# Wider logit and list products, the first slot's turn placed behind the newest logits, and 16 more routing steps ahead of it

## The chip, the cores and the metric

One core of a Trainium2 chip. The metric is the device time of one execution in microseconds, as the median of repeated runs; before the change it is 1103.21 us (three runs, 1103.02 to 1106.22).

## The reference

Two stages. A causal convolution over 8 sequences of 2880 rows of 192 values, with 7 taps that are a softmax of `weight`, one set for each of 8 heads of 24 columns. Then a mixture of experts over the 23040 rows: the group (of 4) with the largest logit, within it the expert (of 4) with the largest logit, the expert's two layers, and the result scaled by both softmax weights.

```python
out = np.einsum('hk,bskhg->bshg', w, x_unf)              # convolution, w = softmax(weight)
g_idx = np.argmax(x @ w_group, axis=1)
e_idx = np.argmax(xg @ w_expert[g], axis=1)
h  = np.maximum(xg[mask_e] @ w1[g, e], 0.0)              # 192 -> 1024
ye = h @ w2[g, e]                                        # 1024 -> 192
out[tok_idx] = (g_w * e_w)[:, None] * ye
```

## The kernel before

**Routing.** The rows are cut into blocks of 120 and the blocks into 18 units (of 4, 8, 12, 8, 8, 8 and then 12 blocks). `unit` is a generator that writes one unit's work stage by stage: eight conv products, one for a head, with a banded matrix as weights (L505); transposes of the convolved rows (L526, L537); the logits (`logits`, L595 and L600); DVE's choice of group and expert; two small products that count rows per expert (L678, L679); one-hot factors `ohl` and `ohv` on DVE; the list product (L725), which sums over the blocks of the unit to a 128 x 32 table of row numbers per expert; and a POOL DMA that writes the table to `idtab` (L731). The last six units take their logits in another way (`logits_thin`, L580). The convolved rows go to `xcd` in HBM.

**Logits.** In `logits(q)`, a quad of four blocks makes two groups of products: one of the last 64 columns of two blocks against 2 x 20 router weights (L595), and for each of the two blocks one of its first 128 columns against 20 (L600). All the logits of a unit lie in one PSUM bank `lp` (20 columns a block), and DVE reads them by a maximum (L638) and a difference (L639).

**Slots.** A slot runs up to 256 (later up to 384) rows of one expert through its two layers. `gather` (L813) fetches the rows named in the table to `xg`; `turn` transposes them on PE (L831, L833), and makes a high half `xa[:, 0]` on ACT (L844, L847) and a low half `xa[:, 1]` on DVE (L848, L851). `hidden` is the first layer: per pair of 128-column pieces ten products (L864), a high half on ACT (`hh`, L869) and a low half on DVE (`hl`, L870). `back` is the second layer (L882, L886), `finish` scales and writes the rows out.

**Order.** `step()` advances the oldest of the running units by one stage. First, steps are taken until five units are routed; then the first table is read and slots 0 and 1 are gathered (`open_slot`), `AHEAD` more steps are written, then the turn of slot 0, and then the loop over the slots, in which `advance` mixes in steps at a rate that is worked out from the steps already done. The framework's scheduler puts the instructions of each engine into a final order from the order written, priorities and simulated times; engines work through their queues in that order. `tc.high_priority` raises what is written inside it, and `tc.issue_after(ins)` places it behind another instruction in that order.

Of the kernel before, what the change touches and what calls it, by code (L numbers as in the profile page):

```python
# [20 lines left out]
P = 128  # L21
BT = 120
# [5 lines left out]
LH = 32  # L28
# [7 lines left out]
def conv_moe_kernel(  # L36
# [10 lines left out]
    nc = tc.nc  # L47
# [26 lines left out]
    NL = G + E  # L74
# [21 lines left out]
    for b in range(B):  # L96
        k = b * NB
# [14 lines left out]
    QGA = 0  # L112
    QGL = 5
    QGB = 3
    AHEAD = 96
    LISTLAG = 8
    LISTLAG0 = 2
    HOLD = 4
# [207 lines left out]
    for g in range(NSK):  # L326
        nc.sync.dma_start(
            out=skew[0:R, g * HG:(g + 1) * HG],
# [17 lines left out]
    for h in range(H):  # L346
        nc.scalar.activation(
            out=band[0:R, h, 0:BT], in_=skew[0:R, h, BT - 1::-1], func=AF.Exp, bias=wm[0:R, h:h + 1],
# [6 lines left out]
    wr = const.tile([P, 3, NL], F32, name="wr")  # L355
# [20 lines left out]
    def widen_weights():  # L376
# [9 lines left out]
        out=tri, in_=ones, pattern=[[1, P]], compare_op=ALU.is_gt, fill=0.0, base=0, channel_multiplier=-1,  # L386
# [10 lines left out]
    for nb in sorted({n for _, n in units}):  # L397
# [32 lines left out]
        out=sel[:, 0:E], in_=ident.rearrange("p (e l) -> p e l", e=E), axis=AX.X, op=ALU.add)  # L430
    nc.gpsimd.iota(io[:, 0:1], pattern=[[0, 1]], base=0, channel_multiplier=1)
    nc.vector.tensor_scalar(
        out=io[:, 1:2], in0=io[:, 0:1], scalar1=LE - 1, scalar2=None, op0=ALU.bitwise_and)
# [8 lines left out]
        out=eold[:, :, E:E + 1], in_=goff.unsqueeze(1).broadcast_to([P, NU + 1, 1]))  # L442
# [15 lines left out]
    def gaps(u):  # L458

        return tuple(UG[4 * u:4 * u + 4]) if 4 * u < len(UG) else (GA, GL, GB, REST)  # L460
# [17 lines left out]
    def unit(u, pre=None):  # L478
        c0, nb = units[u]
# [3 lines left out]
        def bank(kind=None):  # L483
            if BK and kind and len(unit_banks) > 1:
                pool, nm = BKS[BK][kind]
                return pool.tile([P, 512], F32, name=nm)
            npool[0] += 1
            pool, nm = unit_banks[npool[0] % len(unit_banks)]
            return pool.tile([P, 512], F32, name=nm)
# [10 lines left out]
        for h in range(H):  # L500
            if h:
# [4 lines left out]
                out=ps[0:CW, 0:nb * HC], lhsT=band[0:R, h, 0:CW], rhs=xin[0:R, :, c0h:c1h], start=True, stop=True))  # L506
# [79 lines left out]
        lps = []  # L586

        def logits(q):
            if not lps:
                lps.append(bank("l"))  # L590
            lp = lps[0]
            ta, tb = parts[q][:, 0:QN], parts[q][:, QN:QN + QN // 2]
            for i in range(QB // 2):
                b = q * QB + 2 * i
                nc.tensor.matmul(  # L595
                    out=lp[0:BT, b * NL:(b + 2) * NL], lhsT=tb[:, i * BT:(i + 1) * BT],
                    rhs=wr[:, 1:3].rearrange("p k n -> p (k n)"), start=b == 0, stop=False,
                )
                for k in range(2):
                    nc.tensor.matmul(  # L600
                        out=lp[0:BT, (b + k) * NL:(b + k + 1) * NL], lhsT=ta[:, (2 * i + k) * BT:(2 * i + k + 1) * BT],
                        rhs=wr[:, 0], start=False, stop=b + k == nb - 1,
                    )

        ga, gl, gb, rest = gaps(u)
        events = {}
        for q in range(NQ):
            if thin:
                tl = 1 + APART * q
                todo = ((tl, parts_a), (tl + 1, parts_b), (tl + 4, cross), (tl + 4 + CROSS, logits_thin))  # L610
            else:
                tl = ga + gl + 2 * (NQ - 1) + q
                todo = ((ga + 3 * q, turn_a), (ga + 1 + 3 * q, turn_b), (tl, logits))
            for k, f in todo:
                events.setdefault(k, []).append((f, q))
# [5 lines left out]
        Q = BT  # L621
# [6 lines left out]
        if not thin:  # L628
# [12 lines left out]
            out=sc, in0=dd, scalar=0.0, in1=prio[0:Q].unsqueeze(1).broadcast_to([Q, M, EG]),  # L641
# [5 lines left out]
        ohv = oh.rearrange("p (b m) e -> p b m e", m=NG)  # L647
# [3 lines left out]
            out=ohx[0:Q], in0=ohv[:, :, 1:NG, :].rearrange("p b g e -> p g e b"),  # L651
# [36 lines left out]
        with nc.allow_low_precision(reason="small whole numbers, summed in float32"):  # L688
            nc.vector.tensor_reduce(out=pn[0:Q], in_=pos[0:Q].rearrange("p e b -> p b e"), axis=AX.X, op=ALU.add)
        nc.vector.tensor_scalar(  # L690
            out=posi[0:Q, 0], in0=pn[0:Q], scalar1=LH.bit_length() - 1, scalar2=None, op0=ALU.logical_shift_right)
# [3 lines left out]
        ohl = pa.tile([P, UB // 2, P, 2], BF16, name="ohl", bufs=1)  # L695
        ohr = rt.tile([P, UB // 2, LH, 2], BF16, name="ohr", bufs=1)
        ohv = rt.tile([P, UB // 2, LH, 2], F16, name="ohv")

        def wide(a, n):
# [3 lines left out]
            out=ohr[0:Q, 0:nb // 2], in0=ior[0:Q].unsqueeze(1).broadcast_to([Q, nb // 2, LH, 2]),  # L703
# [3 lines left out]
            out=ohv[0:Q, 0:nb // 2], in0=ohr[0:Q, 0:nb // 2],  # L707
# [3 lines left out]
            out=ohl[0:Q, 0:nb // 2], in0=iop[0:Q].unsqueeze(1).broadcast_to([Q, nb // 2, P, 2]),  # L711
# [10 lines left out]
            yield  # L722
        pl = bank("l")
        for b in range(nb):
            nc.tensor.matmul(out=pl[:, 0:LH], lhsT=ohl[0:Q, b // 2, :, b % 2], rhs=ohv[0:Q, b // 2, :, b % 2], start=b == 0, stop=b == nb - 1)  # L725
        none = rt.tile([P, LH], F32, name="none", bufs=1)
        lsi = rt.tile([P, LH], I32, name="lsi", bufs=4)
        nc.vector.tensor_scalar(out=none, in0=pl[:, 0:LH], scalar1=0.0, scalar2=float(BIG), op0=ALU.is_equal, op1=ALU.mult)
# [1 line left out]
            out=lsi, in0=pl[:, 0:LH], scalar=float(t0 + IDB), in1=none, op0=ALU.add, op1=ALU.add)  # L730
        nc.gpsimd.indirect_dma_start(  # L731
            out=TABV, out_offset=bass.IndirectOffsetOnAxis(ap=rowi.bitcast(U32), axis=0), in_=lsi, in_offset=None,
# [3 lines left out]

    loads = []
    lows = []

    def weights(r1, r2, eng=None, held=False):  # L740
        eng = eng or {}
# [78 lines left out]
    def turn(got, w=SLOT):  # L820
        xs, side = got
        rows = xs.rearrange("p t d -> p (t d)")
        n = -(-w // P)
        xa = ff.tile([P, 2, WMAX], F32R, name="xa")
        xb = xbs[nturn[0] % 2]
        nturn[0] += 1
        px = pm.tile([P, 512], F32, name="pm")
        py, o = (px, SLOT) if n <= 2 else (pm.tile([P, 512], F32, name="pm"), 0)
        for t in range(n):
            a = t * XW + (D2 if side and t == 1 else 0)  # L830
            nc.tensor.transpose(px[:, t * P:(t + 1) * P], rows[:, a:a + P], ident)  # L831
            if not side:
                nc.tensor.transpose(py[0:D2, o + t * P:o + (t + 1) * P], xs[:, t, WB:XW], ident)  # L833
            elif t == 1:
                nc.tensor.transpose(py[:, o:o + P], rows[:, WB:WB + P], ident)
            elif t == 2:
                nc.tensor.transpose(py[0:D2, o + P:o + 2 * P], xs[:, t, WB:XW], ident)
        if side:
            parts = [(0, P, py[0:D2, o:o + P], 0), (P, P, py[D2:P, o:o + P], D2)]
            if w > SLOT:  # L840
                parts.append((SLOT, w - SLOT, py[0:D2, o + P:o + P + w - SLOT], 0))
        else:
            parts = [(0, w, py[0:D2, o:o + w], 0)]
        nc.scalar.activation(out=xa[:, 0, 0:w], in_=px[:, 0:w], func=AF.Copy)  # L844
        for c, k, pb, _ in parts:
            for h in (0, D2):
                nc.scalar.activation(out=xb[h:h + D2, 0, c:c + k], in_=pb, func=AF.Copy)  # L847
        nc.vector.tensor_tensor(  # L848
            out=xa[:, 1, 0:w], in0=px[:, 0:w], in1=xa[:, 0, 0:w].bitcast(F32), op=ALU.subtract)
        for c, k, pb, h in parts:  # L850
            nc.vector.tensor_tensor(  # L851
                out=xb[0:D2, 1, c:c + k], in0=pb, in1=xb[h:h + D2, 0, c:c + k].bitcast(F32), op=ALU.subtract)
        return xa, xb
# [276 lines left out]
    def step():  # L1130

        if routed[0] < NU and len(live) < lead[1] and (not live or max(live, key=lambda a: a[0])[1] >= (lead[0] and lead[0] + (SKEWX if routed[0] > THIN else 0) or SK[min(routed[0], len(SK)) - 1])):
            u = routed[0]
            live.append([u, 0, unit(u, xin0 if u == 0 else None)])
            routed[0] += 1
        if not live:
            return
        done[0] += 1
        cur = live.pop(0)
        cur[1] += 1  # L1140
        try:
            next(cur[2])
            live.append(cur)
        except StopIteration:
            pass
# [103 lines left out]
    opened, gathered, turned = {}, {}, {}  # L1249
# [36 lines left out]
    k = 0  # L1286
# [13 lines left out]
    for e in range(2, 2 + PRE2):  # L1300
        pre[e] = weights(e * D, e * F)
    for k in range(AHEAD):
        step()
# [5 lines left out]
        split_one(opened[0][0])  # L1309
    unit_banks[:] = [(pm, "pm")]  # L1310
    lead[:] = SKEW2, LIVE2
    turned[0] = turn(gathered[0])
    pinned[0] = False
    pend = []
    ends = []
# [68 lines left out]
    for i, (pi, e, s) in enumerate(plan):  # L1384
# [13 lines left out]
        for f2 in range(NF // 2):  # L1398
            last = f2 == NF // 2 - 1
# [66 lines left out]
```

## Time and profile before

| | before |
|---|---|
| median of the runs (three) | 1103.21 us |
| the profiled execution's own time | 1095.27 us |
| its span, first to last instruction | 1093.5 us |
| mean granted clock of TensorE | 0.98 |
| PE busy | 1054.8 us (96%) |
| weight loads (PEld) busy | 1027.2 us (94%) |
| DVE busy | 746.6 us (68%) |
| ACT busy | 668.4 us (61%) |
| POOL busy | 524.3 us (48%) |

The profile shows one execution; engines run side by side, so busy times don't add up. "PEclk" is the granted clock as a share of 2.4 GHz: 0.50 is 1.2 GHz. In a row of instructions in time order, the number in brackets is how long the engine stood idle before it and what ended that.

### The profile page before, as it was taken

What the parts mean: (1) busy time and instruction counts of PE and PEld (TensorE: products, weight loads), DVE (VectorE), ACT (ScalarE), POOL (GpSimd) and SP (SyncE); (2) the same over time, 40 slices, a digit from 0 to 9 for tenths busy, and PEclk for the clock granted to TensorE, in tenths of its full rate; (3) what the DMA queues carried; (4) which work ended last, traced back from release to release, by engine and by line L of the source; (5) the groups of instructions that cost most, each with busy time, mean ns of one, the idle gap of its engine ahead of it and who ended that gap; (6) DMA issues with size and microseconds to landing.
All of it is one profiled execution on the core that took longest, in us unless ns stands there. A gap on an engine that the chain in (4) does not pass through costs nothing. (4 is left out here: it accounts for less than half of the span.)

```text
span 1093.5 us, 22348 instructions
## 1 busy us (share of the span) xinstructions
PE 1054.8 (96%) x7908; PEld 1027.2 (94%) x7908; DVE 746.6 (68%) x1790; ACT 668.4 (61%) x1486; POOL 524.3 (48%) x485
## 2 busy tenths in 40 slices
PE   5988999988999999999999999999999999999996
PEld 5868899988999999999999999999999999999996
DVE  3664887888797887886876665656666656566553
ACT  5454676666576666566667665666566656566552
POOL 2014133344455464565555656455555645465432
PEclk9977899999999999999999999999999999999999
DMA  8999679898797785655645432423333332323210
GB/s 186 239 208 245 147 172 222 210 213 221 172 229 179 172 188 107 142 146 129 121 114 130 127 102 81 110 71 101 103 92 101 100 93 73 91 80 100 62 31 26
DMA packets 193540, 148.55 MB, mean 136 GB/s; under 512 B 84635, under 2 KB 178883, under 8 KB 193422
## 3 DMA queue, kind: packets, MB, share of 16 engines
q1 hardware_dynamic: 127392, 92.90, 35.0%
q0 software_dynamic: 19392, 36.09, 12.9%
q10 hardware_dynamic: 46638, 18.07, 7.9%
q8 instruction: 63, 1.03, 0.4%
q14 instruction: 55, 0.45, 0.1%
HBM read 100.48 MB, written 36.47 MB: 125 GB/s over the span
## 5 line engine op out<-in xcount | busy, mean ns | idle before, releaser
L882 PE MATMUL po<-cw,hh 128*128 128x384 f32 x944 | 295.5, 370 | 0.4 <-ACT ys L940 0.4
L864 PE MATMUL ph<-xa,ah 128*128 128x256 f32 x944 | 260.5, 297 | 7.1 <-DVE hl L870 4.7
L869 ACT ACTIVATE hh<-ph 128x512 fp32r<-128x512 f32 x236 | 140.4, 597 | 179.3 <-PE ph L864 158.8
L886 PE MATMUL po<-cw,hl 128*128 128x192 f32 x944 | 237.1, 251 | 0.0
L870 DVE SCALAR_TENSOR_TENSOR hl<-ph,hh 128x512 fp32r<-128x512 f32 x236 | 161.0, 687 | 106.9 <-ACT hh L869 105.1
L813 POOL DMA_INDIRECT xg<-xcd,idpt x137 | 145.4, 1061 | 176.3 <-ACT ys L940 74.3
L813 POOL DMA_INDIRECT xg<-xcd,idp x116 | 131.8, 1136 | 189.7 <-ACT ys L940 94.9
L864 PEld LDWEIGHTS ph<-xa,ah 128*128 128x128 f32 x944 | 179.5, 190 | 10.9 <-DVE hl L870 5.5
L864 PE MATMUL ph<-xb,bb 128*128 128x256 f32 x944 | 189.6, 283 | 0.0
L886 PEld LDWEIGHTS po<-cw,hl 128*128 128x128 f32 x944 | 180.8, 192 | 1.6
L882 PEld LDWEIGHTS po<-cw,hh 128*128 128x128 f32 x944 | 178.3, 189 | 2.2 <-ACT ys L940 0.6
L864 PEld LDWEIGHTS ph<-xb,bb 128*128 128x128 f32 x944 | 146.5, 191 | 0.0
L948 POOL DMA_INDIRECT out<-ys,idpt x99 | 110.0, 1111 | 58.0 <-DVE ys L947 33.3
L864 PE MATMUL ph<-xa,al 128*128 128x256 f32 x472 | 134.7, 285 | 0.0
L948 POOL DMA_INDIRECT out<-ys,idp x88 | 110.4, 1255 | 37.9 <-issue 14.9
L902 PE MATMUL ph<-xa,ah 128*128 128x384 f32 (+1 forms) x368 | 122.1, 334 | 0.8 <-DVE spare L908 0.5
L940 ACT ACTIVATE ys<-po,xg 128x384 f32<-128x384 f32 x164 | 93.0, 583 | 35.4 <-PE po L886 14.5
L847 ACT ACTIVATE xb<-pm 64x128 fp32r<-64x128 f32 (+2 forms) x342 | 95.3, 279 | 3.4 <-DMA xcd<-xc 0.3
L864 PEld LDWEIGHTS ph<-xa,al 128*128 128x128 f32 x472 | 90.0, 191 | 1.9
L902 PE MATMUL ph<-xb,bb 128*128 128x384 f32 (+1 forms) x368 | 90.2, 326 | 0.0
L947 DVE TENSOR_TENSOR ys<-ys 128x192 f32<-128x192 f32 x179 | 62.1, 357 | 29.5 <-ACT ys L940 26.3
L783 DVE TENSOR_TENSOR cw<-raw,cw 128x768 fp32r<-128x768 f32 x80 | 76.1, 953 | 8.9 <-ACT cw L782 8.6
(260 smaller groups left out, 2141.4 us busy)
## 6 DMA issues: line engine op xcount, KB each, us to landing
raw<-in_moe_w SPq DMA_DIRECT2D x80, 384.0 KB
raw<-in_moe_w SPq DMA_DIRECT2D x40, 512.0 KB
raw<-in_moe_w SPq DMA_DIRECT2D x40, 256.0 KB
xcd<-xc ACTq DMA_DIRECT2D x12, 742.5 KB
xin<-in_x SPq DMA_DIRECT2D x7, 1134.0 KB
xin<-in_x SPq DMA_DIRECT2D x6, 1039.5 KB
xcd<-xcb ACTq DMA_DIRECT2D x13, 360.0 KB
xg<-xcd,idpt POOLq DMA_INDIRECT x137
```

What stands on the lines that cost most here:

```text
L783: eng.get(k, nc.vector).tensor_tensor(out=cw[:, fs, 1, :], in0=rc[k - 2], in1=cw[:, fs, 0, :].bitcast(F32), op=ALU.subtract,)
L813: ins = nc.gpsimd.indirect_dma_start(out=rows[0:n, to:to + size], out_offset=None, in_=xcd[0:known, :], in_offset=bass.IndirectOffsetOnAxi ...
L847: nc.scalar.activation(out=xb[h:h + D2, 0, c:c + k], in_=pb, func=AF.Copy)
L864: nc.tensor.matmul(out=hp[:, j], lhsT=wgt[:, fs], rhs=xx, start=i == 0, stop=i == len(ops) - 1)
L869: nc.scalar.activation(out=hh, in_=hp, func=AF.Relu)
L870: lows.append(nc.vector.scalar_tensor_tensor(out=hl, in0=hp, scalar=0.0, in1=hh.bitcast(F32), op0=ALU.max, op1=ALU.subtract,))
L882: nc.tensor.matmul(out=oo[t][:, 0:2 * D], lhsT=hh[:, j, ts], rhs=cw[:, f].rearrange("p a d -> p (a d)"), start=f == 0, stop=False,)
L886: nc.tensor.matmul(out=oo[t][:, 0:D], lhsT=hl[:, j, ts], rhs=cw[:, f, 0, :], start=False, stop=f == NF - 1,)
L902: nc.tensor.matmul(out=hp[:, 0:w], lhsT=wgt[:, fs], rhs=xx, start=i == 0, stop=i == len(ops) - 1)
L940: nc.scalar.activation(out=y, in_=oo[t][0:n, 0:2 * D], func=AF.Copy, scale=g)
L947: nc.vector.tensor_tensor(out=y[:, 0:D], in0=y[:, 0:D], in1=y[:, D:2 * D], op=ALU.add)
L948: nc.gpsimd.indirect_dma_start(out=outviews[nscat[0] % len(outviews)], out_offset=bass.IndirectOffsetOnAxis(ap=ids[t].bitcast(U32), axis=0 ...
```

## The change

Each logit product streams its 20 or 40 router columns several times (three times in units of 4 and 8 blocks, twice in units of 12: as often as a bank of 512 columns allows, three at most), into copies beside each other in the same bank, of which the first is read as before. Each list product streams its 32 columns three times in the same way. `scored` keeps the last logit product of each quad; the turn of slot 0 gets priority and is placed behind the newest of these. `AHEAD` goes from 96 to 112.

```diff
-    AHEAD = 96
+    AHEAD = 112
...
-            lp = lps[0]
+            reps = min(3, 512 // (nb * NL))
+            lp = lps[0][:, 0:reps * nb * NL].rearrange("p (k n) -> p k n", k=reps)
...
                 nc.tensor.matmul(
-                    out=lp[0:BT, b * NL:(b + 2) * NL], lhsT=tb[:, i * BT:(i + 1) * BT],
-                    rhs=wr[:, 1:3].rearrange("p k n -> p (k n)"), start=b == 0, stop=False,
+                    out=lp[0:BT, :, b * NL:(b + 2) * NL], lhsT=tb[:, i * BT:(i + 1) * BT],
+                    rhs=wr[:, 1:3].rearrange("p k n -> p (k n)").unsqueeze(1).broadcast_to([P, reps, 2 * NL]),
+                    start=b == 0, stop=False,
                 )
                 for k in range(2):
-                    nc.tensor.matmul(
-                        out=lp[0:BT, (b + k) * NL:(b + k + 1) * NL], lhsT=ta[:, (2 * i + k) * BT:(2 * i + k + 1) * BT],
-                        rhs=wr[:, 0], start=False, stop=b + k == nb - 1,
+                    last = nc.tensor.matmul(
+                        out=lp[0:BT, :, (b + k) * NL:(b + k + 1) * NL],
+                        lhsT=ta[:, (2 * i + k) * BT:(2 * i + k + 1) * BT],
+                        rhs=wr[:, 0].unsqueeze(1).broadcast_to([P, reps, NL]), start=False, stop=b + k == nb - 1,
                     )
+            scored.append(last)
...
-            nc.tensor.matmul(out=pl[:, 0:LH], lhsT=ohl[0:Q, b // 2, :, b % 2], rhs=ohv[0:Q, b // 2, :, b % 2], start=b == 0, stop=b == nb - 1)
+            nc.tensor.matmul(
+                out=pl[:, 0:3 * LH].rearrange("p (k n) -> p k n", k=3), lhsT=ohl[0:Q, b // 2, :, b % 2],
+                rhs=ohv[0:Q, b // 2, :, b % 2].unsqueeze(1).broadcast_to([Q, 3, LH]), start=b == 0, stop=b == nb - 1)
...
+    scored = []
...
-    turned[0] = turn(gathered[0])
+    with tc.high_priority(), tc.issue_after(scored[-1].ins):
+        turned[0] = turn(gathered[0])
```

The change moves instructions on PE and DVE at the first slot. On PE before, from the last product of unit 5's list, over the turn of slot 0 (`xg_246`, two tiles), to the first products of the hidden layer (`xa`, `ah`, `al`); L505 is a conv product, L595 and L600 are logits:

```order
L725 MATMUL ph<-ohv,ohl 128x32
L831 MATMUL pm<-ident,xg_246 128x128
L833 MATMUL pm<-ident,xg_246 64x128
L831 MATMUL pm<-ident,xg_246 128x128
L833 MATMUL pm<-ident,xg_246 64x128
L505 MATMUL pm<-xin,band 120x288
L595 MATMUL pm<-wr,ta 120x40
L600 MATMUL pm<-wr,ta 120x20 x2
L595 MATMUL pm<-wr,ta 120x40
L600 MATMUL pm<-wr,ta 120x20
L864 MATMUL ph<-xa,ah 128x256
L864 MATMUL ph<-xa,al 128x256
```

And now, from the last logits ahead of the turn to the first hidden product (its lines are 7 higher there, L838 for L831, L871 for L864):

```order
L602 MATMUL ph<-wr,ta 120x2x20 x2
L838 MATMUL pm<-ident,xg_246 128x128
L840 MATMUL pm<-ident,xg_246 64x128
L838 MATMUL pm<-ident,xg_246 128x128
L840 MATMUL pm<-ident,xg_246 64x128
L505 MATMUL po<-xin,band 120x288
L596 MATMUL ph<-wr,ta 120x2x40
L602 MATMUL ph<-wr,ta 120x2x20 x2
L596 MATMUL ph<-wr,ta 120x2x40
L602 MATMUL ph<-wr,ta 120x2x20 x2
L505 MATMUL pm<-xin,band 120x288
L871 MATMUL ph<-xa,ah 128x256
```

Before, the turn came straight behind unit 5's list and all six groups of unit 8's logits behind it, mixed with hidden products; now two conv products and four of the six groups stand between that list and the turn, two groups behind it, and none among the hidden products. From unit 8's list product on, the numbers of conv, logit, hidden and back products ahead of each list product are the same in both orders (five rows later in the new one).

On DVE before, where the low half of slot 0 (`xa`, `xb_242`) is made; L638 and L639 are the maximum and the difference over a unit's logits:

```order
L646 TENSOR_TENSOR oh<-sc,mx 120x240
L666 SCALAR_TENSOR_TENSOR se<-se,sg 120x12
L667 RECIPROCAL xc<-se 120x12x4
L638 TENSOR_REDUCE mx<-pm 120x60
L639 TENSOR_TENSOR dd<-pm,mx 120x240
L640 SCALAR_TENSOR_TENSOR sc<-dd,prio 120x240
L645 TENSOR_REDUCE mx<-sc 120x60
L848 TENSOR_TENSOR xa<-pm,xa 128x256
L851 TENSOR_TENSOR xb_242<-pm,xb_242 64x256
```

And now:

```order
L696 TENSOR_SCALAR posi<-posn 120x12
L642 TENSOR_REDUCE mx<-ph 120x60
L698 CAST posh<-posi 120x24
L721 TENSOR_TENSOR rows<-eold,sel 128x17
L643 TENSOR_TENSOR dd<-ph,mx 120x240
L855 TENSOR_TENSOR xa<-pm,xa 128x256
L858 TENSOR_TENSOR xb_242<-pm,xb_242 64x256
L706 TENSOR_TENSOR ohr<-ior,posh 120x384
L714 TENSOR_TENSOR ohl<-iop,posh 120x1536
```

The low half still stands behind the maximum over unit 8's logits; two operations on those logits that stood ahead of it are now behind it, and the position steps of unit 6 (from the counts to `posi`) have come ahead of it.

## Rows read from the trace of the kernel before

**Rows 1.** Stretches of the span: busy time of each engine, granted clock, DMA share, GB/s

```profile
core 0: us, PE busy (x) PEld busy (x) DVE busy (x) ACT busy (x) POOL busy (x), PEclk, DMA share, GB/s
...
52.00:58.90 6.90, 6.90 (x41) 5.82 (x41) 3.74 (x19) 2.47 (x7) 0.97 (x1) 0.51 0.80 190
...
62.30:65.70 3.40, 3.40 (x12) 2.57 (x11) 2.40 (x5) 1.14 (x3) 0.00 (x0) 0.51 1.01 175
...
75.90:79.30 3.40, 3.40 (x12) 2.49 (x11) 0.00 (x0) 2.42 (x7) 0.68 (x1) 0.51 1.12 234
...
93.00:117.00 24.00, 21.14 (x102) 18.88 (x101) 11.49 (x40) 6.06 (x15) 8.41 (x9) 0.50 0.68 173
117.00:220.00 103.00, 102.96 (x828) 98.64 (x828) 86.55 (x209) 71.25 (x147) 34.99 (x29) 1.00 0.84 203
220.00:300.00 80.00, 72.80 (x627) 70.03 (x626) 66.01 (x146) 46.96 (x97) 38.38 (x30) 0.98 0.94 200
```

**Rows 2.** PE in order of time, logit groups: start us, us, line, operation

```profile
90.44 0.38 PE L595 MATMUL ph<-wr,ta 128*120 128x40 f32 x2
90.65 0.57 PE L600 MATMUL ph<-wr,ta 128*120 128x20 f32 x4
91.07 0.38 PE L595 MATMUL ph<-wr,ta 128*120 128x40 f32 x2
...
106.91 0.60 PE L595 MATMUL pm<-wr,ta 128*120 128x40 f32 x2
...
108.11 0.60 PE L595 MATMUL pm<-wr,ta 128*120 128x40 f32 x2
```

**Rows 3.** PE in order of time, the turn and the first hidden products of slot 0

```profile
100.14 0.45 PE L831 MATMUL pm<-ident,xg 128*128 128x128 f32 x1 [2.12 <-DMA xg<-xcd,idp]
...
101.11 0.48 PE L831 MATMUL pm<-ident,xg 128*128 128x128 f32 x1 [0.31 <-DMA xg<-xcd,idp]
...
110.51 0.56 PE L864 MATMUL ph<-xa,ah 128*128 128x256 f32 x1
```

**Rows 4.** DVE in order of time, the wait ahead of slot 0's low half

```profile
110.71 0.41 DVE L638 TENSOR_REDUCE mx<-pm 120x60 f32<-120x240 f32 x1 [9.13 <-PE pm L600]
...
112.36 0.41 DVE L848 TENSOR_TENSOR xa<-pm,xa 128x256 fp32r<-128x256 f32 x1
```

**Rows 5.** POOL in order of time, from the last table write to the first gather

```profile
84.03 1.66 POOL L1192 DMA_DIRECT2D idp<-idtab  x2 [7.44 <-DMA idtab<-lsi,rowi]
92.08 1.09 POOL L813 DMA_INDIRECT xg<-xcd,idp  x1 [6.39 <-DMA idp<-idtab]
```

**Rows 6.** PE in order of time at full clock: transposes, conv, hidden, back and list products

```profile
86.63 0.57 PE L526 MATMUL pm<-ident,spare 120*128 120x120 f32 x4
87.04 0.65 PE L505 MATMUL pm<-xin,band 126*120 126x288 f32 x2
87.53 0.65 PE L505 MATMUL po<-xin,band 126*120 126x288 f32 x2
...
163.84 0.28 PE L864 MATMUL ph<-xa,ah 128*128 128x256 f32 x1
163.96 0.40 PE L864 MATMUL ph<-xb,bb 128*128 128x256 f32 x2
...
164.37 0.25 PE L886 MATMUL po<-cw,hl 128*128 128x192 f32 x1
164.46 0.36 PE L882 MATMUL po<-cw,hh 128*128 128x384 f32 x1
...
167.13 0.47 PE L725 MATMUL pm<-ohv,ohl 120*128 120x32 f16 x12
167.45 0.42 PE L882 MATMUL po<-cw,hh 128*128 128x384 f32 x1
```

**Rows 7.** Who PE waited for from 220 to 300 us: total, times, longest

```profile
PE ph L864 <- DVE hl L870: 3.3, 2, 1.9
PE pm L580 <- DMA ta<-spare: 2.5, 2, 1.4
```

**Rows 8.** Sum over the stretches from 90 to 150 us, columns as in rows 1

```profile
sum 60.00, PE 57.13 PEld 53.24 DVE 44.98 ACT 28.98 POOL 18.89; mean PE 9.52 PEld 8.87 DVE 7.50 ACT 4.83 POOL 3.15
```

## The prediction, made blind

> **What bounds the kernel now.** I read the page first: its slices show TensorE (PE) busy almost everywhere and the granted clock below full speed only early on. The table of stretches then says where. From 117 to 220 us PE is busy 102.96 of 103 us at full clock, while VectorE (DVE) and DMA have room [rows 1]: from there on the time is PE's own work, and whatever lets PE arrive at 117 us earlier is kept unless a later wait takes it back. Ahead of it lie four stretches at 1.2 GHz: 52.0 to 58.9, 62.3 to 65.7, 75.9 to 79.3 and 93 to 117 us, 37.7 us together [rows 1]. The last is the dear one: 24.0 us, of which PE counts 21.14 as busy.
>
> What does PE do there? A group of logit products (one with 40 columns and two with 20, for two blocks) takes 0.63 us at full clock (90.44 to 91.07) and 1.20 at half (106.91 to 108.11) [rows 2]. The clock fell at about 93 us behind four such groups in a row, with no idle time. So a busy PE alone did not keep it; few columns against many weight loads is what stands there. The two earlier stretches that ended soonest hold conv products.
>
> PE's rows at the first slot [rows 3] and DVE's [rows 4] show a second fault. PE waits 2.12 us for the gathered rows, turns them at 100.14 and 101.11, then works through unit 8's six logit groups at half clock until 110.51. DVE's queue has the maximum over those logits ahead of the slot's low half `xa`: it stands still for 9.13 us, and the low half comes at 112.36 though the second tile was turned at 101.11. Three things meet: half clock, logits in between, DVE in order behind them.
>
> **The gathered rows' own chain** is a DMA one: table written, 7.44 us of waiting for it, ids loaded, 6.39 us, first gather at 92.08 [rows 5], usable at 100.14. It is only as early as units 0 to 4 are routed.
>
> **The change, part by part.** The sum is made against the profiled execution, 1095.27 us (span 1093.5); the median of the runs is 1103.21, 7.9 us above, and I subtract the same gain from it.
>
> *Wider logit products.* A product is bound by its weight load: 2 instructions in 0.21 us, for 40 columns (90.44 to 90.65) as for 20 [rows 2]. A conv product of 288 columns takes 0.49 us [rows 6], so 120 columns stream in 0.20 us and 80 in 0.14: below 0.21, so they cost nothing; the cover is the weight load, and without it the 40 to 80 added columns would cost 0.07 to 0.14 us a product.
>
> *The stretch 93 to 117.* Its PE work at full-clock prices: 12 transposes at 0.10 (four in 0.41) 1.2, eight logit groups at 0.63 5.0, a list product of 8 blocks 0.2, the turn 0.4, three conv products at 0.49 1.5, 19 hidden products at 0.12 2.3 [rows 6], two small counts 0.1: 10.7 us, where it now takes 24.0. Against these 13.3 us stand waits that then show. With the change two conv products and four logit groups lie ahead of the turn: from 93.0 they, the transposes, two groups of unit 7 and the list make 6.3 us, so PE is at the turn at 99.3. The two tiles come at 100.1 and 101.1, which costs 0.8 and 0.8 us. Then conv, two groups, conv (2.3) to 103.6, and four hidden products on the high half to 104.1. The low half on DVE follows the maximum and the difference of unit 8's logits, now complete at 103.1: 104.4 at the earliest, 105.7 if unit 6's some twenty position steps ahead of them run one after another. I take 105.2, a wait of 1.1. So 13.3 less 2.7: 10.6, call it 10.5. The 16 steps are worth only this reordering: past unit 8's list the PE order is the same again, so no work leaves the kernel and nothing is added to any queue; on POOL unit 7's table write moves ahead of the fifth slot's gather, at a place where POOL is idle.
>
> *The first two stretches at half clock* (6.9 and 3.4 us) cost PE 5.1 us. How much of that moves the chain of the gather forward is unknown: none if its DMAs or DVE set it, all 5.1 if PE does. PE waits for DVE between them, so I take 2. The third follows a PE wait for DVE and stays.
>
> *Wider list products.* Twelve blocks of 32 columns take 0.32 us (167.13 to 167.45), 27 ns each. No row has 96 columns after a bf16 weight load; nearest is a product of 192 columns, 0.09 us (164.37 to 164.46) [rows 6]: half of it is 45 ns. So 12 x 18 ns = 0.2 us a unit, and the 12 units listed in the full main loop lose 2.4 us. Ends: 0 (if the load is what counts) and 6.5 (if the whole 45 ns come on top).
>
> *The later stage.* From 220 to 300 us PE is idle 7.2 us [rows 1], for DVE's low halves and for transposing DMAs [rows 7]. Its order does not change; I enter 0, with ends of -7 and +2.
>
> Sum: 10.5 + 2.0 - 2.4 = 10.1 us faster: 1085.2 for a profile like the one shown, 1093.1 for the median. The bounds give 1087.6 (5.1 for the early stretches, lists free), and 1085 if the new waits also vanish.
>
> **Rivals.** *The clock falls at 93 us all the same, 1101.0 us.* Unit 7's groups are mixed with 18 transposes, and in the trace the fall comes just among them. That is the change not doing what it says at the place where it matters. Priced at half clock: twice 6.3 us to the turn (105.6), 0.8 for the turn, 4.4 for the rows behind it, 4.6 for 19 hidden products, less a conv product done ahead (1.0): the state of 117.0 is reached at 114.4. That gains 2.6, with 2.0 and -2.4 as above 2.2. For it: the fall among the transposes. Against it: the groups get twice the columns, and the stretches that ended had transposes in them as well.
> The Trainium skill, "TensorE: Matmul & The Clock Gate", section "Part 4: PE-mode transpose", says that transposes do not count as PE activity in the same way and do not bring the full clock. By that rule this rival is the right one, and the time would be 1101.0; the rows of this case leave it open, since no stretch here holds transposes alone.
>
> *A later stage takes part of it back, 1098 us.* PE comes to 220 us ten us earlier, the transposing DMAs and DVE do not: half of the gain, 5 us, goes into waits there. For it: DVE is busy 66 of 80 us and the DMA share is 0.94 in that stretch [rows 1]. Against it: DMA stood at a share of 0.68 before 117 us, so loads wait for buffers rather than the other way round.
>
> *Slower, 1112.7 us: DVE becomes the bound of the first slots.* It is busy 44.98 of the 60 us from 90 to 150 [rows 8]; 9.13 of the idle time is the wait that goes. With ten us taken out, PE's hidden products wait for DVE's low halves. Four waits of the longest size now seen, 1.9 us [rows 7], and the clock at half once more for 24 us (12 lost) turn the forecast into 1093.1 + 7.6 + 12.0. It decides from where such waits come close enough together for the clock to fall inside the slots. Against it: from 117 to 220 us DVE is busier still (86.55 of 103) and PE hardly waits [rows 1].
>
> **How the numbers follow.** A measurement of this kernel can tell about 0.3%, 3.3 us, from no change: 1099.9 to 1106.5. The forecast (1085 to 1097) has 0.60; the clock that falls at 93 all the same 0.20, mostly within 0.3%; the later stage 0.13, faster in most of its spread; DVE as the bound 0.07. So faster 0.60 + 0.05 + 0.10 = 0.75, same 0.15 + 0.03 = 0.18, slower 0.07. The range goes from the best bound, 1085, to 1102, which takes in the second case and the third.
>
> **What would show it.** Right: a granted clock near 1.0 from 93 to 110 us; the first turn near 100 us with logit groups of 0.63 us on both sides; the DVE wait of 9 us gone and the low half within 4 us of the turn; hidden products in an unbroken row from about 105; list products of twelve blocks at about 0.5 us. Wrong: a clock of 0.5 behind the transposes of unit 7; PE idle at the first slots in waits for DVE's `hl`; the idle time between 220 and 300 us grown from 7.2 to over 10; list products that take over 0.6 us.

## The result and the profile after

The change is slower: 1120.16 us (median of 6 runs, 1112.44 to 1123.45) against 1105.61 us for the kernel before beside it (6 runs), a ratio of 1.0108 [1.0083, 1.0134] (here and below the bracket is a 95% interval, and a ratio is taken over the runs and not from the medians, which give 1.0132). The prediction was 1093.1 us, range 1085 to 1102. Two repeats on other chips, where before ran at 1090 and 1089 us, gave 1.0055 [1.0031, 1.0079] and 1.0070 [1.0042, 1.0098]: smaller, slower all the same.

| | after |
|---|---|
| the profiled execution's own time, and its span | 1121.33 us, 1119.6 us |
| mean granted clock of TensorE | 0.98 |
| PE busy | 1062.4 us (95%) |
| weight loads (PEld) busy | 1032.8 us (92%) |
| DVE, ACT, POOL busy | 747.6, 663.4, 528.1 us |

The view of stretches of the changed kernel, columns as in [rows 1]:

```profile
core 0: us, PE busy (x) PEld busy (x) DVE busy (x) ACT busy (x) POOL busy (x), PEclk, DMA share, GB/s
57.40:64.60 7.20, 6.89 (x35) 5.71 (x36) 4.31 (x21) 3.31 (x6) 0.97 (x1) 0.53 1.01 227
78.00:82.00 4.00, 4.00 (x20) 3.01 (x18) 1.26 (x7) 2.04 (x6) 0.96 (x1) 0.57 1.03 223
93.00:117.00 24.00, 19.07 (x138) 17.01 (x138) 16.56 (x59) 8.24 (x23) 10.57 (x9) 0.90 1.01 226
109.00:112.00 3.00, 3.00 (x13) 2.70 (x13) 2.44 (x7) 0.00 (x0) 0.00 (x0) 0.50 1.12 263
117.00:132.60 15.60, 13.57 (x116) 12.58 (x115) 11.34 (x32) 10.25 (x22) 0.98 (x1) 0.93 0.66 156
132.60:149.20 16.60, 16.60 (x79) 16.45 (x78) 9.33 (x29) 5.84 (x9) 5.92 (x5) 0.51 0.38 115
220.00:300.00 80.00, 72.07 (x597) 68.51 (x595) 65.09 (x141) 47.46 (x99) 36.18 (x28) 0.98 0.98 205
```

From 93 to 117 us the clock is 0.90 where it was 0.50, near the forecast; it is at half again from 109 to 112 us. But PE is busy for only 19.07 us there (21.14 before, at half the speed), the DMA share has gone from 0.68 to 1.01, and a new stretch at half clock stands inside the first slots, at 132.6 to 149.2 us, where before had 1.00 [rows 1].

PE of the changed kernel in order of time: the last groups of unit 7's logits with its transposes, the turn of slot 0, and the first hidden products:

```profile
94.82 0.61 PE L526 MATMUL pm<-ident,xc 120*128 120x120 f32 x4
...
96.15 0.34 PE L596 MATMUL ph<-wr,ta 128*120 128x80 f32 x2
...
96.71 0.41 PE L596 MATMUL ph<-wr,ta 128*120 128x80 f32 x2
...
97.89 0.37 PE L537 MATMUL pm<-ident,xcb 120*128 120x120 f32 x2
...
102.12 0.30 PE L838 MATMUL pm<-ident,xg 128*128 128x128 f32 x1
...
105.50 0.49 PE L871 MATMUL ph<-xa,ah 128*128 128x256 f32 x1
...
108.37 0.36 PE L871 MATMUL ph<-xa,ah 128*128 128x256 f32 x1 [2.25 <-DVE dd L643]
...
114.81 0.38 PE L871 MATMUL ph<-xa,ah 128*128 128x256 f32 x1 [2.00 <-ACT xc L510]
```

A group of logits takes 0.56 us at 96.15, at full clock and with twice the columns (0.63 and 1.20 in [rows 2]). The turn comes at 102.12 without a wait for its rows (100.14 in [rows 3]). But hidden products that started at 105.50 stop twice, and behind the first stop the clock falls. That stop, 2.25 us, ends as DVE comes to the low half (108.14, below): the third product of a pair is the first that reads it, and the bracket names the operation just ahead of it on DVE. It is the wait that the prediction put at 1.1. The second stop is new in kind; ACT of the changed kernel in order of time shows it:

```profile
102.58 0.32 ACTq L675 DMA_DIRECT2D xcd<-xc  x1
...
114.35 0.41 ACT L510 ACTIVATE xc<-ph 120x288 f32<-120x288 f32 x1 [8.26 <-DMA xcd<-xc]
...
115.53 0.63 ACT L876 ACTIVATE hh<-ph 128x512 fp32r<-128x512 f32 x1
```

ACT stands for 8.26 us until a write of convolved rows to `xcd`, issued at 102.58, has landed: unit 9's rows go into the buffer that unit 6's are written from. Slot 0's `hh` is queued behind this copy and three more of unit 9's. ACT of the kernel before in order of time:

```profile
112.10 0.40 ACT L644 ACTIVATE dd<-dd 120x240 f32<-120x240 f32 x1 [8.35 <-DVE sc L640]
112.41 0.39 ACT L510 ACTIVATE xc<-pm 120x288 f32<-120x288 f32 x1
...
115.36 0.60 ACT L869 ACTIVATE hh<-ph 128x512 fp32r<-128x512 f32 x1 [1.92 <-PE ph L864]
```

So the slot's first high half is no earlier than it was. At half clock PE itself needed until then: ACT waited for it, and for DVE, and its first copy of unit 9's rows (112.41) shows no wait for the write.

DVE of the changed kernel in order of time, at slot 0's low half and ahead of unit 7's list:

```profile
107.33 0.41 DVE L642 TENSOR_REDUCE mx<-ph 120x60 f32<-120x240 f32 x1 [1.76 <-PE pm L505]
...
108.14 0.41 DVE L855 TENSOR_TENSOR xa<-pm,xa 128x256 fp32r<-128x256 f32 x1
...
127.43 1.21 DVE L778 TENSOR_TENSOR al<-raw,ah 128x1024 fp32r<-128x1024 f32 x1
...
128.83 1.22 DVE L782 TENSOR_TENSOR bb<-raw,bb 64x1024 fp32r<-64x1024 f32 x1
130.08 0.36 DVE L706 TENSOR_TENSOR ohr<-ior,posh 120x384 bf16<-120x384 f16 x1
130.36 0.95 DVE L714 TENSOR_TENSOR ohl<-iop,posh 120x1536 bf16<-120x1536 f16 x1
131.23 0.35 DVE L710 TENSOR_TENSOR ohv<-ohr,idl 120x384 f16<-120x384 bf16 x1
```

The wait of 9.13 us [rows 4] is down to 1.76, and the low half comes at 108.14 instead of 112.36. Further on both halves of a weight split (`al`, `bb`, 2.4 us) stand right ahead of unit 7's one-hot factors, for which PE waits, in the changed kernel's PE rows:

```profile
120.41 0.70 PE L729 MATMUL pm<-ohv,ohl 120*128 120x96 f16 x12
120.93 0.36 PE L871 MATMUL ph<-xa,ah 128*128 128x256 f32 x1
...
131.63 0.69 PE L729 MATMUL pm<-ohv,ohl 120*128 120x96 f16 x12 [2.03 <-DVE ohv L710]
```

The half-clock stretch begins right behind this wait.

### The profile page after: what moved, and what is told of

Its sections match the earlier page's. It is cut to its first block, busy times and chain, and to the rows that moved or that the text cites. A ratio compares the mean times of both kernels' runs of the same rounds, so it can differ in the third digit from the quotient of the medians.

```text
span 1119.6 us, 22352 instructions
## 1 busy us (share of the span) xinstructions
PE 1062.4 (95%) x7908; PEld 1032.8 (92%) x7908; DVE 747.6 (67%) x1790; ACT 663.4 (59%) x1486; POOL 528.1 (47%) x485
## 5 line engine op out<-in xcount | busy, mean ns | idle before, releaser
L871 PE MATMUL ph<-xa,ah 128*128 128x256 f32 x944 | 262.5, 298 | 12.0 <-DVE hl L877 5.2
L820 POOL DMA_INDIRECT xg<-xcd,idp x116 | 136.3, 1175 | 192.5 <-ACT ys L947 94.6
L871 PEld LDWEIGHTS ph<-xa,ah 128*128 128x128 f32 x944 | 181.5, 192 | 17.2 <-DVE hl L877 6.4
L871 PE MATMUL ph<-xb,bb 128*128 128x256 f32 x944 | 192.6, 286 | 0.0
L871 PEld LDWEIGHTS ph<-xb,bb 128*128 128x128 f32 x944 | 148.9, 193 | 0.3 <-issue 0.2
L871 PE MATMUL ph<-xa,al 128*128 128x256 f32 x472 | 135.5, 287 | 0.8 <-issue 0.8
L871 PEld LDWEIGHTS ph<-xa,al 128*128 128x128 f32 x472 | 90.7, 192 | 2.0 <-issue 0.3
```

The source lines that it names most:

```text
L820: ins = nc.gpsimd.indirect_dma_start(out=rows[0:n, to:to + size], out_offset=None, in_=xcd[0:known, :], in_offset=bass.IndirectOffsetOnAxi ...
L871: nc.tensor.matmul(out=hp[:, j], lhsT=wgt[:, fs], rhs=xx, start=i == 0, stop=i == len(ops) - 1)
```

## The experiments

Times are medians; each ratio is to before, run beside it on the same chip.

**1. Halves of the change.** Theory A: the order at the first slot does the harm. Theory B: the wider products do it.

`wide_both`: the change with

```diff
-    AHEAD = 112
+    AHEAD = 96
...
-    with tc.high_priority(), tc.issue_after(scored[-1].ins):
-        turned[0] = turn(gathered[0])
+    turned[0] = turn(gathered[0])
```

> Only the wider logit and list products; AHEAD 96 and the turn of the first slot as before. Theory A (the order at the first slot does the harm: conv outputs and DMAs of later units stand in ACT's queue ahead of the slot's first hidden layer, PE waits and its clock falls inside the slots): within 0.4% of before, 1100 to 1110 us, no half-clock stretch between 120 and 160 us. Theory B (the wider products do it: lists dearer, and the prologue's order that follows from them delays units 2 to 4): 1113 to 1122 us, the chain's last table write at about 79 us as in the changed kernel, and most of the loss there.

Measured: 1.0028 [1.0003, 1.0053].

`order_both`: before with the other two edits, the products as narrow as before:

```diff
-    AHEAD = 96
+    AHEAD = 112
...
-    turned[0] = turn(gathered[0])
+    with tc.high_priority(), tc.issue_after(scored[-1].ins):
+        turned[0] = turn(gathered[0])
```

> Only AHEAD 112 and the turn with priority behind the newest logits; products as narrow as before. Theory A: 1113 to 1122 us, ACT waiting some 8 us for a DMA of unit 6 ahead of the conv outputs that stand before the first hidden layer. Theory B: 1100 to 1108 us.

Measured: 1.0013 [0.9985, 1.0041].

`ahead_only`: the first of these two pieces alone.

> Only AHEAD 112. If the 16 steps alone put the conv outputs ahead of the first slot's work on ACT (theory A in its narrower form), 1110 us or more; if the turn's place is what matters, within 0.4% of before.

Measured: 1.0017 [0.9989, 1.0046].

`turn_only`: the second alone.

> Only the turn's priority and its place behind the newest logits, AHEAD 96. Theory A in its narrower form (the 16 steps do it): within 0.4% of before, or up to 5 us faster since DVE's wait of 9 us in front of the low half gets shorter. If the turn's place does it: 1110 us or more.

Measured: 0.998 [0.9956, 1.0005]. What follows: no half has the whole loss; neither theory holds as it stood.

**2. One kind of wider product taken out.** `after_again` is the change, `before_again` the kernel before, as a control and for a profile on that chip.

> The changed kernel once more, beside the kernel before on the same chip. If its parts add up (0.28% and 0.13% alone, neither clear of noise), the ratio is 1.002 to 1.006. If the parts together do what neither does alone, the ratio is again 1.008 or more. If the loss belonged to the chip of the first measurement, the ratio is within 0.3% of 1.

Measured: 1.0055 [1.0031, 1.0079].

> The kernel before, for a profile on the same chip: ratio 1.000. If the profiles shown so far came from unlike conditions, its milestones lie up to 8 us away from those of the first profile, in small steps over the whole span.

Measured: 0.9991 [0.9973, 1.001].

`logits_order`: the change with the list product of before.

```diff
-            nc.tensor.matmul(
-                out=pl[:, 0:3 * LH].rearrange("p (k n) -> p k n", k=3), lhsT=ohl[0:Q, b // 2, :, b % 2],
...
+            nc.tensor.matmul(out=pl[:, 0:LH], lhsT=ohl[0:Q, b // 2, :, b % 2], rhs=ohv[0:Q, b // 2, :, b % 2], start=b == 0, stop=b == nb - 1)
```

> The change without the wider list products. Theory: the loss comes of wider logits and the new order together, lists cost 0.2 us a unit: about 2 us less than the changed kernel, ratio 1.005 to 1.010. If the lists are what hurts together with the order: within 0.3% of before.

Measured: 0.9986 [0.997, 1.0003].

`lists_order`: the change with the logit products of before, of which the core is

```diff
-            reps = min(3, 512 // (nb * NL))
-            lp = lps[0][:, 0:reps * nb * NL].rearrange("p (k n) -> p k n", k=reps)
+            lp = lps[0]
```

> The change without the wider logit products. Theory: within 0.3% of before plus 2 us for the lists, ratio 1.000 to 1.004. If the lists are what hurts together with the order: 1.008 or more.

Measured: 1.0077 [1.0049, 1.0105].

What follows: taking the wider lists out gives back 7.6 us (`after_again` to `logits_order`), three times the 2.4 of the forecast. Without them the rest gains next to nothing, though the clock is better (a mean of 0.990 over the runs, 0.984 before).

**3. Two mechanisms, tried one by one.** The order on DVE shows what the lists change beside their length. The rows ahead of unit 7's list in `logits_order` (L776 and L780 are the split):

```
L776 TENSOR_TENSOR al<-raw,ah 128x1024
L706 TENSOR_TENSOR ohr<-ior,posh 120x384
L714 TENSOR_TENSOR ohl<-iop,posh 120x1536
L710 TENSOR_TENSOR ohv<-ohr,idl 120x384
L780 TENSOR_TENSOR bb<-raw,bb 64x1024
```

And in the change (L778, L782), word for word as in `lists_order` but for line numbers:

```
L778 TENSOR_TENSOR al<-raw,ah 128x1024
L698 CAST posh<-posi 120x24
L723 TENSOR_REDUCE rowi<-rows 128x1
L782 TENSOR_TENSOR bb<-raw,bb 64x1024
L706 TENSOR_TENSOR ohr<-ior,posh 120x384
L714 TENSOR_TENSOR ohl<-iop,posh 120x1536
L710 TENSOR_TENSOR ohv<-ohr,idl 120x384
```

`after_late` puts that one instruction back; `ohvs[u]` keeps each unit's `ohv`, `nbb` counts the splits:

```diff
+                nbb[0] += 1
+                with tc.issue_after(ohvs[7].ins) if nbb[0] == 3 and 7 in ohvs else nullcontext():
...
                     eng.get(k, nc.vector).tensor_tensor(
                         out=bb[D2:P], in0=rb[0:D2], in1=bb[0:D2].bitcast(F32), op=ALU.subtract)
```

> The whole change, with one DVE instruction moved: of the third weight split the low half of `bb` (1.22 us) stands behind unit 7's one-hot factors instead of ahead of them. Theory C (the wider list products change the scheduler's times so that this split comes ahead of unit 7's factors; PE then waits 2.0 us for `ohv` inside the first slots, and the clock stands at half behind it for 17 us): the wait ahead of unit 7's list is about 1 us, no half clock from 129 to 147 us, and the time is that of the change without wider lists (0.9986 of before) plus 12 units at 0.2 us, so a ratio of 1.0008, 1.000 to 1.002. Theory D (the wider list products cost 7 us themselves, wherever DVE's instructions stand): 1.0055 as with the whole change.

Measured: 1.0042 [1.0018, 1.0066], between the two theories. The wait ahead of unit 7's list was 0.70 us, and the clock stayed at 1.00 behind it.

`room_late` is `logits_order` with that edit, and another buffer for unit 9:

```diff
-            xc = room_tile(0 if u >= THIN - 3 else None)
+            xc = room_tile(0 if u >= THIN - 2 else None)
```

> The change without wider lists, with unit 9's convolved rows in another buffer (one that unit 5 left free) and the same split behind unit 7's factors. Theory E (the gain of the full clock at the first slot goes into ACT's wait for a buffer, 8.75 us until the write of unit 6's rows to HBM has landed, with slot 0's `hh` queued behind it): ACT does not stand there, slot 0's first `hh` comes at about 104 to 105 us where it came at 110.5, and 4 to 5 us are gained: ratio 0.995. Rival F (the DMA engines, at a share above 1 from 94 to 110 us, are the bound: another transfer is late in its place): `hh` earlier, but PE waits as long for loads or gathered rows within the next 30 us, and the ratio stays at 0.9986.

Measured: 0.9969 [0.9941, 0.9997].

`after_both`: the whole change with both edits.

> The whole change with both edits: the split behind unit 7's factors and the other buffer for unit 9. Theories C and E together: 1.0008 less 0.004, so 0.997. C with F: 1.0008. D with F: 1.0055.

Measured: 1.0002 [0.9975, 1.003], 4.6 us less than `after_late` (1102.17 against 1106.76). The buffer gains with the wider lists too.

`wide_lists`: before with the wider lists alone.

> Before with the wider list products alone. In this kernel the order on DVE leaves the split away from unit 7's factors. Theory C: only the streaming, 12 units at 0.2 us and a little in the first six: 2.4 to 3 us, ratio 1.0022 to 1.0028. Theory D: 5 us and more, ratio 1.005 to 1.007.

Measured: 1.0054 [1.0033, 1.0074]. Here the split does not stand at unit 7's factors, and the lists cost 0.54%, 5.9 us (7.2 between the medians), all the same: theory C is not the whole of it. The profile shows two PE waits for DVE, 1.07 us at 123.31 and 1.25 at 141.51, that the profiles of before don't have at these places.

**4. All on one chip.** `third_after` is the change again.

> The exact change, as the measure for the next three on the same chip. Both theories: slower than before, ratio 1.004 to 1.011.

Measured: 1096.68 us, 1.0070 [1.0042, 1.0098].

`late_split` is `after_late` again.

> The whole change with the third weight split's `bb` behind unit 7's factors. Theory C (place of the split): 4 us and more below the exact change. Theory D (the lists themselves): within 2 us of the exact change.

Measured: 1092.71 us, 1.0035 [1.0015, 1.0055]: 4.0 us less, with an interval of -1.2 to 7.9 (here and below from resampling the runs). So the split's share is likely, but not shown.

`logits_late` is `logits_order` with the split's edit.

> The same without the wider list products (logits, turn and 16 steps, split behind unit 7's factors): 2.4 to 3.2 us below late_split if the lists cost only their streaming (48 blocks of the first six units and 144 of the later ones at 17 ns: 3.2 us); 5 us and more below if they cost something else too.

Measured: 1087.85 us, 0.9988 [0.9969, 1.0007]: 4.9 us less [3.1, 7.3]. So the lists have a cost of their own, apart from the split. Whether it is more than the 3.2 us of streaming is not shown on this chip, since the interval reaches down to 3.1.

`room_again` is `room_late` again.

> logits_late with the free buffer for unit 9's rows. Theory E (ACT's wait for the write of unit 6's rows holds the first slot): 2 to 4 us below logits_late. Rival F (another transfer is late in its place): within 1 us of it.

Measured: 1080.80 us (6 runs), 0.9921 [0.9892, 0.995]: 7.0 us less [1.1, 9.2]. Theory E holds in its direction; the 2 to 4 us that it forecast lie within the interval.

The time of each run splits into what the half clock takes, time x (1 - mean granted clock), and the rest (work and waits, as if at full clock). Means on this chip, rough to some tenths, since the mean clock covers idle time too:

| | time | clock | lost to the clock | rest |
|---|---|---|---|---|
| before (28 runs) | 1089.7 | 0.9828 | 18.8 | 1070.9 |
| third_after (11) | 1096.6 | 0.9869 | 14.4 | 1082.3 |
| late_split (12) | 1093.8 | 0.9892 | 11.9 | 1082.0 |
| logits_late (12) | 1088.0 | 0.9901 | 10.8 | 1077.2 |
| room_again (6) | 1082.5 | 0.9928 | 7.8 | 1074.7 |

So the change does win clock time, 4.4 us. It adds 11.4 us of work and waits. By these means, moving the split changes the clock's part alone; taking the lists out saves 4.8 us of the rest; the buffer saves 2.5 of the rest and 3.0 of the clock.

How the buffer's wait goes can be read in the traces. First ACT of `logits_late` in order of time:

```profile
93.69 0.32 ACTq L675 DMA_DIRECT2D xcd<-xc  x1
...
105.24 0.41 ACT L510 ACTIVATE xc<-ph 120x288 f32<-120x288 f32 x1 [9.72 <-DMA xcd<-xc]
...
106.42 0.63 ACT L878 ACTIVATE hh<-ph 128x512 fp32r<-128x512 f32 x1
```

and PE of the same kernel, which was at its hidden products 8 us earlier:

```profile
97.63 0.35 PE L873 MATMUL ph<-xa,ah 128*128 128x256 f32 x1 [0.39 <-DVE dd L643]
...
105.70 0.58 PE L873 MATMUL ph<-xa,ah 128*128 128x256 f32 x1 [5.19 <-ACT xc L510]
```

**5. The version that beats both.** `room_third` is `room_late` again; `before_room` is before with the buffer's edit alone.

> The change without wider lists, with the split behind unit 7's factors and the free buffer for unit 9's rows. Theory E: below before by what the two earlier runs bracket, a ratio of 0.992 to 0.997.

Measured: 1084.45 us, 0.9955 [0.9934, 0.9976].

> Before with the free buffer for unit 9's rows alone. Theory E: nothing is gained, since PE works at half clock there and ACT does not stand for that write: ratio 0.998 to 1.002. Rival G (the buffer gains whatever the clock does): 0.995 or less.

Measured: 1090.41 us, 1.0012 [0.999, 1.0034]. The buffer is worth nothing at half clock. The gain of `room_third` needs both. A second kernel at half clock agrees: in `order_both` ACT stands 3.15 us for the same write, until 109.08, and slot 0's first `hh` at 111.10 still waits for PE (0.70 us).

ACT of `room_third` in order of time: the write is issued at 97.26, and unit 9's first rows no longer wait for it.

```profile
97.26 0.32 ACTq L675 DMA_DIRECT2D xcd<-xc  x1
...
99.04 0.41 ACT L510 ACTIVATE spare<-ph 120x288 f32<-120x288 f32 x1
...
103.40 0.60 ACT L878 ACTIVATE hh<-ph 128x512 fp32r<-128x512 f32 x1 [2.38 <-PE ph L873]
```

The view of stretches, 93 to 117 us, in `before_again`:

```profile
93.00:117.00 24.00, 22.15 (x116) 19.48 (x117) 11.42 (x39) 7.95 (x21) 4.12 (x5) 0.64 0.56 144
```

in `logits_late`:

```profile
93.00:117.00 24.00, 18.10 (x120) 15.56 (x120) 12.41 (x46) 9.86 (x24) 3.99 (x4) 0.86 0.84 206
```

and in `room_third`:

```profile
93.00:117.00 24.00, 23.07 (x192) 21.02 (x189) 20.52 (x72) 14.71 (x35) 6.80 (x7) 1.00 1.01 239
```

In the same 24 us PE gets through 116 instructions at clock 0.64, then 120 at 0.86 with 5.9 us idle, then 192 at 1.00 with 0.9. The second row is the change's clock without a place for its rows; the third is what the prediction had in mind. It is the best of three profiles of this kernel. The same stretch in `room_again` and in `room_late`:

```profile
93.00:117.00 24.00, 21.28 (x141) 18.60 (x139) 14.37 (x53) 9.83 (x26) 8.54 (x9) 0.79 0.84 213
```

```profile
93.00:117.00 24.00, 21.27 (x154) 18.95 (x153) 16.00 (x57) 10.48 (x27) 8.95 (x9) 0.86 0.96 234
```

There PE waits for the gathered rows ahead of the turn, 1.98 us until 99.20 and 1.45 until 99.08, and the clock falls about there. In `room_third` PE has no wait above 0.4 us in this stretch.

## Why the prediction was wrong

**The stretch 93 to 117, 10.5 us: the clock right, the waits wrong.** The full clock came and held until about 109 us: groups of 0.56 to 0.63 us on both sides of the turn, the turn at 102.12, DVE's wait down to 1.76. What failed is the step "a wait of 1.1" after which hidden products run on unbroken. The sum has 2.7 us of waits in this stretch; PE stood still for 4.9 (24.00 less 19.07), and the clock fell beside two of the waits, which the sum puts at nothing. I priced DVE's queue and left out ACT's: slot 0's `hh` stands there behind unit 9's conv outputs, and these behind the write of unit 6's rows. That nothing is added to any queue was wrong there: four of these outputs stand ahead of the first `hh`, where before had two. The wait was invisible in the trace of before, because PE at half clock came later than the write. Measured, the rest of the time grew by 6.3 us from before to `logits_late` (1070.9 to 1077.2), against a gain of 8.0 us in the clock's part: 1.7 us are left. The other buffer won 5.5 us in the means, 7.0 in the medians.

**Wider list products, 2.4 us: the step that failed most.** The streaming was as forecast: a list of 12 blocks went from 0.32 us to 0.52 (120.41 to 120.93, and [rows 6]), 17 ns a product. I left out the 48 blocks of the first six units, with which it is 3.2 us. Measured on one chip it is 8.8 us together: 4.9 of their own, and 4.0 that went with the split on DVE, a share whose interval takes in nothing. The prediction said of the later order that nothing moves past unit 8's list, and had compared it on PE alone. On DVE the wider lists shift the scheduler's times: `bb` stands ahead of unit 7's factors in the change and in `lists_order`, and behind them in `logits_order`. What the lists cost beyond their streaming, 1.6 us in the table's rest and 2.7 in `wide_lists`, isn't settled.

**The first two stretches, 2.0 us:** not seen. The changed kernel still has 7.2 us at clock 0.53 and 4.0 at 0.57 early on, and its turn is 2.0 us later than in [rows 3]. Profiles of one and the same kernel differ as much there: the turn of before comes at 100.14 in the first profile and at 94.42 in `before_again`.

**The later stage, entered as 0: right.** PE is idle for 7.9 us from 220 to 300, and was for 7.2 [rows 1]. The changed kernel doesn't come there earlier, so it is no test of the rival that sees the gain taken back there; `room_third` comes earlier, and PE is idle for 1.9 us in the same stretch.

**The rivals.** That the clock falls at 93 all the same is refuted: it held through 18 transposes of unit 7, the last two at 97.89. By the Trainium skill, "TensorE: Matmul & The Clock Gate", section "Part 4: PE-mode transpose", which has transposes not count as PE activity in the same way, that fall was to be expected. The trace doesn't agree in the outcome; but wide logits stand between the transposes, and no run here has transposes alone. The rival that ended slower, at 0.07, came nearest: PE waits for DVE inside the first slots, and in three of four profiles the clock falls behind such a wait. It named the wrong wait, `hl` for `ohv`, and gave it too small a chance. Its objection, that DVE was busier still later on without harm, didn't hold: what PE waited for here was one operation (`ohv`), with two others (`al`, `bb`) ahead of it.

**What stays open.** Why the first measurement, at 1.0108, lies above the repeats. Its profile has single waits of up to 1.29 us in the main loop, put down to "issue", which the first profile of before hasn't. The four profiles from the chip where before ran at 1100 us (`after_late`, `room_late`, `after_both`, `wide_lists`) have such waits too, and no other profile has: they look like the chip's own, but a profile of before on either of these chips is lacking. And 3.8 us of the rest between `room_again` and before were not traced to a place.

## What to carry to other kernels

A stretch at half clock can hide a wait that is shorter than the time it loses. Before counting on the clock's return, walk each queue that the stretch feeds, at full-clock times, to the next transfer or buffer that must be free: here that was a copy on ACT waiting for a write to HBM. Where a scheduler orders by simulated times, longer instructions reorder engines that the edit does not touch, so compare the order on all of them, at every place where PE waits.

## What the runs showed of the hardware

**The clock decides from run to run.** Ten executions of `after_again` took 1091.1 to 1101.5 us; time x mean granted clock lay between 1080.2 and 1082.3 in all of them. Nearly all of the spread is clock.

**The same wait did not always bring the clock down.** In four profiles of kernels with the split ahead of unit 7's factors, PE waits 2.02 or 2.03 us ahead of that list. Behind it the clock was at half for 17 us in `after` and `after_again`, for about 3 in `lists_order`, and not at all in `third_after`. The view of stretches, 130 to 146 us, in `after_again`:

```profile
130.00:146.00 16.00, 16.00 (x76) 15.85 (x76) 8.77 (x27) 5.99 (x9) 5.92 (x5) 0.50 0.35 105
```

and in `third_after`, with its list's row from PE in order of time:

```profile
130.00:146.00 16.00, 15.40 (x121) 14.41 (x119) 13.68 (x30) 10.18 (x20) 6.76 (x7) 1.00 0.63 168
```

```profile
123.64 0.69 PE L729 MATMUL pm<-ohv,ohl 120*128 120x96 f16 x12 [2.02 <-DVE ohv L710]
```

Where that wait was 0.70 to 0.97 us (nine profiles of kernels with the split behind the factors), the clock stayed up behind it. In the two long stretches unit 9's wide logits, mixed with hidden products, follow the fall, and PE is busy throughout. Nor does such a stretch need that wait: in `turn_only` and `ahead_only`, with narrow products, the clock was at half for about 10 and 7 us here, and no wait of PE in the 8 us ahead was above 0.8 us. The view of `turn_only`:

```profile
130.00:140.50 10.50, 10.50 (x51) 10.50 (x51) 5.20 (x14) 2.98 (x4) 2.90 (x3) 0.52 0.46 140
```

**What stood beside the falls at the first slot.** In three profiles with narrow logits (`before`, `order_both`, `lists_order`) the clock fell with PE busy, behind four groups in a row, at 93, 90 and 89 us. In three others (`before_again`, `before_room`, `wide_lists`) it fell only during the wait for the gathered rows (4.34 us until 94.42 in `before_again`). In the eleven profiles with wide logits and the new order it never fell behind unit 7's groups with PE busy. In ten of them it fell later in this stretch, during a PE wait of 0.7 to 5.2 us or within 1 us of one; in `room_third`, which has no such wait, it did not fall. That fits the width doing what it was meant to do and the waits then taking the clock, which the sum priced as idle time alone.
